# A third bank for the first layer, cutoff tests on ScalarE, and search counts summed by TensorE

## The chip, the cores and the metric

The kernel runs on one core of a Trainium2 chip. The core has TensorE (PE, matrix multiply; its weight loads are listed as PEld), VectorE (DVE), ScalarE (ACT), GpSimd (POOL) and SyncE (SP, which only issues DMAs here). PSUM, where TensorE leaves its results, is used as eight banks of 128 x 512 floats. The metric is the device time of one execution in microseconds (us); less is better. Three runs of the kernel before gave 1374.98, 1375.17 and 1376.15 us.

## What is computed

```python
def _attn_ref(x, weight):                 # x: 8 x 3584 x 192, weight: 8 heads x 7 taps
    w = softmax(weight, axis=-1)
    # causal sum over the 7 last positions, one set of taps for each group of 24 columns
    out = np.einsum('hk,bskhg->bshg', w, x_unf)

def _moe_ref(x, w_gate, w1, w2):          # x: 28672 x 192, 8 experts, F = 1024
    logits = x @ w_gate
    order = np.argsort(-logits.flatten())
    for idx in order:                     # greedy, best logit first
        tok, e = idx // E, idx % E
        if assigned[tok] >= 0 or counts[e] >= cap:   # cap = 3584
            continue
        assigned[tok] = e
        counts[e] += 1
    for e in range(E):
        mask = assigned == e
        h = np.maximum(x[mask] @ w1[e], 0.0)
        out[mask] = h @ w2[e]
```

All values are float32. Every expert gets exactly 3584 tokens, seven tiles of 512, so there are 56 tiles for the two layers.

## The kernel before

**Stages.** First comes the convolution over sixteen half batches (`conv`, `logits`), until about 205 us. After it `FFN.run` (L1321) computes the 56 tiles, and the assignment of tokens to experts is worked out piece by piece beside both.

**One tile.** Tile i goes through eight steps f. In each, `l1` (L1234) makes one block of the hidden layer in a PSUM bank `ph` by five matmuls; ScalarE writes its rounded positive part `hh`, and VectorE the remainder `hl` from the same bank, which is then free. Between the blocks `l2` (L1253) multiplies the `hh` and `hl` of the tile before with the second weights into a bank `y`; `store` (L1267) takes it out by ScalarE (`yt`) and VectorE (`yo`), and POOL scatters it. There are two banks for `ph`, two for `y`, two (`bg`) for the assignment, and two (`pa`, `pd`) for transposed tokens: eight in all.

**Tokens of a tile.** `gather` (L1201) fetches them two tiles ahead. While the assignment isn't finished, `prep` (L1310) has TensorE transpose them in steps 2 and 3 (`transp`, L1211, each call half of the blocks of both banks), and `evac` (L1224) splits them into high and low parts in steps 4 and 5. For a tile that is prepared when the assignment is done (`free`), `shuffle` (L1281) does it on VectorE.

**Assignment.** `half(0)` finds a first threshold and the lists for the first tiles; `half(1)` the second half's lists; `rest` (L1397) takes `open`, then `rounds` (L685), `final` (L803) and the `lists` for the three experts of `ib0`; `last` makes the lists of the other tiles. `rounds` runs seven entries of `ROUNDS` (L283). Each calls `choose` (L659), which tests each logit against a cutoff per expert (eight VectorE operations of 256 columns, one per expert, L668) and picks the best expert left. Then five of the seven rounds search the cutoffs in two passes: a 0/1 table of 8 experts x n thresholds x `nmax` candidates is made, its candidates are added up on VectorE by halving, and one matmul with a matrix of ones adds the partitions (L740 to L755). `choose` runs once more in `final`, so eight times in all.

**What sets the order.** Every engine's order is the program's order, laid down while the kernel is built. The assignment's pieces are Python generators, run one after the other. `Steps.hook` (L92) is called four times in each step f, and puts up to four pieces into the program at that place, unless a running estimate (`Pace`, `Meter`) says that VectorE is more than `slack`, or ScalarE more than `act`, ahead of TensorE, or that the piece waits for an estimated time (`PEW`: VectorE's estimate plus 0.8). In `FFN.run` these bounds are `SS = (0.65, 2)` (L1544).

**Points where the order is forced.** The tiles come as: eight first tiles, one of each expert; sixteen more by the lists `ia`; from tile 24 on by `ib0`, and from tile 27 on by `ib`. A list must be complete in the program before the gather that uses it, two tiles ahead. So `idx_of` (L1528) calls `bg.drain(1)` before tile 24's gather, at the head of i = 22, and `bg.drain()` at the head of i = 25: all pieces that are left up to there are put into the program at once, with no tile between them.

Of the kernel before, what the change touches and what calls it, by code (L numbers as in the profile page):

```python
# [5 lines left out]
F32 = mybir.dt.float32  # L6
BF = mybir.dt.bfloat16
I32 = mybir.dt.int32
FR = mybir.dt.float32r
AF = mybir.ActivationFunctionType  # L10
OP = mybir.AluOpType
AX = mybir.AxisListType
PSUM = bass.MemoryType.PSUM

NE, D, NTOK, F, CAP = 8, 192, 28672, 1024, 3584
W, HW_, NHB = 112, 16, 16
G = 256
# [94 lines left out]
def build(ctx, tc, nc, x, weight, wg, attn, LT, wk):  # L112
# [147 lines left out]
    def logits_t(i):  # L260
# [10 lines left out]
        if not last:  # L271
            V.tensor_tensor(o, o, v[:, 1], op=OP.add)

    k.load, k.conv, k.transp, k.split, k.logits, k.logits_t = load, conv, transp, split, logits, logits_t
    k.toeplitz, k.gate_ops, k.transp_last, k.logits_last = toeplitz, gate_ops, transp_last, logits_last
    return k
# [17 lines left out]
class Route:  # L294
# [364 lines left out]
    def choose(self):  # L659

        V, wk = self.nc.vector, self.wk
        L, t = self.LT, self.t
        us = self.u = [wk.tile([128, 4, G], F32, name="X0"), wk.tile([128, 4, G], F32, name="X1")]
        mu = self.mu = wk.tile([128, G], F32, name="c_mu")
        T = wk.tile([128, 8], F32, name="c_T")
        V.tensor_scalar(T, t, -1.0, None, op0=OP.mult)
        for e in range(8):
            V.scalar_tensor_tensor(us[e // 4][:, e % 4], L[:, e], T[:, e:e + 1], L[:, e], op0=OP.is_lt, op1=OP.subtract)  # L668
            if e % 2:
                yield  # L670
        m = wk.tile([128, 4, G], F32, name="X2")
        for q in range(2):
            V.tensor_tensor(m[:, 2 * q:2 * q + 2], us[0][:, 2 * q:2 * q + 2], us[1][:, 2 * q:2 * q + 2], op=OP.min)
            yield
        V.tensor_tensor(m[:, 0:2], m[:, 0:2], m[:, 2:4], op=OP.min)
        yield
        V.scalar_tensor_tensor(mu, m[:, 0], 0.5, m[:, 1], op0=OP.min, op1=OP.min)
        yield
        nw = self.nw = wk.tile([128, 8, G], BF, name="X2")
        for q in range(4):  # L680
            V.tensor_tensor(nw[:, 2 * q:2 * q + 2], us[q // 2][:, 2 * (q % 2):2 * (q % 2) + 2],
                            mu[:, None, :].to_broadcast([128, 2, G]), op=OP.not_equal)
            yield

    def rounds(self, sched=ROUNDS):  # L685


        nc, wk, cst = self.nc, self.wk, self.cst
        V, A, PE = nc.vector, nc.scalar, nc.tensor
        t = self.t = cst.tile([128, 8], F32, name="T")  # L690
        self.Ts2 = cst.tile([128, 1], F32, name="Ts2")
        V.tensor_scalar(self.Ts2, self.Ts, 1.5, None, op0=OP.mult)
        V.memset(t, 0.25)
        x = wk.tile([128, 8], F32, name="r_x")
# [3 lines left out]
        for parts, beta, exact, nmax in sched:  # L698
# [3 lines left out]
            for q in range(4):  # L702
                for e in range(2 * q, 2 * q + 2):
                    A.activation(wk.tile([128, G], BF, name="a_d"), self.nw[:, e], AF.Copy, accum_out=c[:, e:e + 1])
                u = self.u[q // 2][:, 2 * (q % 2):2 * (q % 2) + 2]
# [13 lines left out]
            ps = self.bg()  # L719
# [8 lines left out]
            if parts:  # L728

                V.tensor_tensor(tl, t, self.Ts2.to_broadcast([128, 8]), op=OP.min)  # L730
                V.tensor_scalar(d, tl, self.Ts, beta, op0=OP.add, op1=OP.mult)
                n = parts - 1
                jd = wk.tile([128, 2, 8, 15], F32, name="X1")[:, :, :, 0:n]
                dd = wk.tile([128, 2, 8], F32, name="r_dd")
                for s in range(2):
                    V.tensor_scalar(dd[:, s], d, float(parts) ** -(s + 1), None, op0=OP.mult)
                    V.tensor_tensor(jd[:, s], self.j1[:, None, 0:n].to_broadcast([128, 8, n]),
                                    dd[:, s, :, None].to_broadcast([128, 8, n]), op=OP.mult)
                yield
                for s in range(2):  # L740
                    th = wk.tile([128, 8, 15], F32, name="m_f")[:, :, 0:n]
                    V.tensor_tensor(th, tl[:, :, None].to_broadcast([128, 8, n]), jd[:, s], op=OP.subtract)
                    g = wk.tile([128, 8, 15, 16], BF, name="X0")[:, :, 0:n]
                    V.tensor_tensor(g[:, :, :, 0:nmax], k[:, :, None, :].to_broadcast([128, 8, n, nmax]),
                                    th[:, :, :, None].to_broadcast([128, 8, n, nmax]), op=OP.is_gt)
                    yield
                    m = nmax // 2
                    while m > 1:
                        V.tensor_tensor(g[:, :, :, 0:m], g[:, :, :, 0:m], g[:, :, :, m:2 * m], op=OP.add)
                        m //= 2  # L750
                    cc = wk.tile([128, 8, 15], BF, name="r_cc")[:, :, 0:n]
                    V.tensor_tensor(cc, g[:, :, :, 0], g[:, :, :, 1], op=OP.add)
                    yield PEW
                    ps = self.bg()[:, 0:8 * n].rearrange("p (e j) -> p e j", j=n)
                    PE.matmul(ps, self.ones, cc, start=True, stop=True)  # L755
                    ok = wk.tile([128, 8, 15], F32, name="m_x")[:, :, 0:n]
                    V.tensor_tensor(ok, ps, x[:, :, None].to_broadcast([128, 8, n]), op=OP.is_le)
                    no = wk.tile([128, 8], F32, name="r_no")
                    V.tensor_reduce(no, ok, axis=AX.X, op=OP.add)
                    V.tensor_tensor(no, no, dd[:, s], op=OP.mult)  # L760
                    V.tensor_tensor(tl, tl, no, op=OP.subtract)
            wl, xr = w[:, :, 0:8], x8
            if parts:
                g = wk.tile([128, 8, 16], BF, name="r_g2")
                V.tensor_tensor(g[:, :, 0:nmax], k, tl[:, :, None].to_broadcast([128, 8, nmax]), op=OP.is_gt)
                cc = wk.tile([128, 8], BF, name="r_c8")
# [6 lines left out]
                ps = self.bg()  # L773
# [15 lines left out]
            ps = self.bg()  # L789
# [8 lines left out]
            ps = self.bg()  # L798
# [42 lines left out]
class General:  # L841
# [9 lines left out]
    def consts(self):  # L851
# [39 lines left out]
        V.tensor_scalar(self.c31, self.c31, 31, None, op0=OP.logical_shift_left)  # L891
        self.T = p.tile([128, 8], F32, name="g_T")
        V.memset(self.T, -3.4028234663852886e38)
        self.I = p.tile([128, 8], F32, name="g_I")
# [8 lines left out]
    def choose(self):  # L903
# [9 lines left out]
        for e in range(8):  # L913
            T, I = self.T[:, e:e + 1], self.I[:, e:e + 1]
            V.tensor_scalar(c, self.id, I, None, op0=OP.is_le)
# [169 lines left out]
class FFN:  # L1085
# [122 lines left out]
                in_offset=bass.IndirectOffsetOnAxis(ap=idx[b], axis=0),  # L1208
                bounds_check=rows - 1, oob_is_err=False)

    def transp(self, i, u):  # L1211

        x = self.XG[i]
        if u == 0:
            self.pa = self.pt.tile([128, 512], F32, name="pa")
            self.pd = self.pt.tile([128, 512], F32, name="pd")
        for b in (2 * u, 2 * u + 1):
            q = slice(128 * b, 128 * b + 128)
            self.nc.tensor.transpose(self.pa[:, q], x[:, b, 0:128], self.ident)
            self.nc.tensor.transpose(self.pd[0:64, q], x[:, b, 128:D], self.ident)  # L1220
        if u:
            self.XG.pop(i)

    def evac(self, i, u):  # L1224

        A, V = self.nc.scalar, self.nc.vector
        if u == 0:
            self.XT[i] = (self.xs.tile([128, 2, 512], FR, name="xa"), self.xs.tile([128, 512], FR, name="xd"))
        xa, xd = self.XT[i]
        hi, lo, p = ((xa[:, 0], xa[:, 1], self.pa), (xd[0:64], xd[64:128], self.pd[0:64]))[u]  # L1230
        A.activation(hi, p, AF.Copy)
        V.tensor_tensor(lo, p, hi.bitcast(F32), op=OP.subtract)

# [76 lines left out]
    def prep(self, i, step):  # L1310

        if i in self.free:
            if step < 7:
                self.shuffle(i, step)
            return
        if step == 2 or step == 3:
            self.transp(i, step - 2)
        elif step == 4 or step == 5:
            self.evac(i, step - 4)

    def run(self, idx_of, at, eng, free):  # L1321

# [29 lines left out]
def moe_kernel(ctx, tc, x, weight, wg, w1, w2, out):  # L1352
    nc = Pace(tc.nc)
    V, P = nc.vector, nc.gpsimd
# [4 lines left out]
    with ExitStack() as cw:  # L1359
        pool = lambda c, name, bufs, **kw: c.enter_context(tc.tile_pool(name=name, bufs=bufs, **kw))  # L1360
        late = dict(reuse_waits="tile")
        right = dict(side="right")
        wk = pool(cw, "wk", 1)
# [4 lines left out]
        r = Route(tc, nc, LT, lst, wk, drm)  # L1368
        r.oh_pool = oh
        r.bg = lambda: bgp.tile([128, 512], F32, name="bg")  # L1370
        ff = FFN(tc, nc, attn, w1, w2, out, r.ident, wr, drm)
# [10 lines left out]
        tiles, n = [], 0  # L1382
# [44 lines left out]
        cs, c1, ct, ca, cl, cc = (ExitStack() for _ in range(6))  # L1427
# [72 lines left out]
        cx[0].close()  # L1500
        cc.close()
        ff.pt = pool(cw, "pt", 1, space=PSUM, **right, **late)
        ff.ph = pool(cw, "ph", 2, space=PSUM, **right, **late)
        bg.drain(5)
        nc.lat, nc.las = (0.8, 1.2)
        gather()
        bg.keep = 0
        ff.xs = pool(cw, "fx", 2, **late)
        for u in range(2):
            ff.transp(0, u)  # L1510
        for u in range(2):
            ff.evac(0, u)
        for _ in range(2):
            ff.wsplit(-1, P)
# [26 lines left out]
                bg.drain()  # L1541
            return [ib[:, e, 4 * (t - 3) + b:4 * (t - 3) + b + 1] for b in range(4)]

        SS = (0.65, 2)  # L1544
        ff.bg = lambda: bg.hook(SS[0], 4, SS[1])

        def at(i):
# [41 lines left out]
```

## Time and profile before

| | |
|---|---|
| median of three runs | 1375.17 us |
| the profiled execution: its time, its span | 1377.14 us, 1375.2 us |
| busy: PE, PEld, DVE | 1288.4, 1106.8, 1046.1 us |
| busy: ACT, POOL | 586.0, 637.0 us |
| mean granted clock of TensorE | 0.964 of full speed |
| HBM read, written | 114.44 MB, 72.35 MB |

Engines work beside each other, so the busy times are not to be added. A busy PE is not one at its peak: its matmuls overlap, and their ends are modelled. Tables by window give, for each stretch of the span, the busy time of each engine with the number of its instructions in brackets, then the granted clock (1.00 is full), the share of the DMA engines and the GB/s. Rows of a timeline begin with start and length, both in us; a bracket at their end is the idle time before them with what ended it. Groups end with busy us, mean ns, and, behind the bar, idle time before them.

### The profile page before, as it was taken

What the parts mean: (1) busy time and instruction counts of PE and PEld (TensorE: products, weight loads), DVE (VectorE), ACT (ScalarE), POOL (GpSimd) and SP (SyncE); (2) the same over time, 40 slices, a digit from 0 to 9 for tenths busy, and PEclk for the clock granted to TensorE, in tenths of its full rate; (3) what the DMA queues carried; (4) which work ended last, traced back from release to release, by engine and by line L of the source; (5) the groups of instructions that cost most, each with busy time, mean ns of one, the idle gap of its engine ahead of it and who ended that gap; (6) DMA issues with size and microseconds to landing.
All of it is one profiled execution on the core that took longest, in us unless ns stands there. A gap on an engine that the chain in (4) does not pass through costs nothing.

```text
span 1375.2 us, 20862 instructions
## 1 busy us (share of the span) xinstructions
PE 1288.4 (94%) x7367; PEld 1106.8 (80%) x7367; DVE 1046.1 (76%) x2216; ACT 586.0 (43%) x1242; POOL 637.0 (46%) x607
## 2 busy tenths in 40 slices
PE   5978897998989999999959999999999999999997
PEld 2545564887879989889848999999999999999997
DVE  7598963777988888888877477777777777777772
ACT  4755473447544434434413433333333333333332
POOL 5655566556754443443403344444444444444432
PEclk9998897999999999999959999999999999999999
DMA  9996568677872443343312152324231414141110
GB/s 231 284 271 166 170 218 286 204 231 248 260 260 83 143 137 97 138 143 118 100 60 81 32 197 89 101 89 139 86 99 49 140 44 146 45 142 42 42 35 28
DMA packets 114431, 188.23 MB, mean 137 GB/s; under 512 B 12352, under 2 KB 86544, under 8 KB 110096
## 3 DMA queue, kind: packets, MB, share of 16 engines
q1 hardware_dynamic: 63888, 120.75, 27.6%
q0 software_dynamic: 21504, 44.07, 10.3%
q10 hardware_dynamic: 28928, 22.02, 4.9%
q8 instruction: 59, 0.97, 0.3%
q14 instruction: 52, 0.43, 0.1%
HBM read 114.44 MB, written 72.35 MB: 136 GB/s over the span
## 4 chain that ended last, share of the span: by engine, by line
PE 74%; DVE 14%; DMA 4%; issue 3%; ACT 2%; POOL 2%; SPq 0%; POOLq 0%; DVEq 0%; ACTq 0%
PE ph L53 34%; PE y L53 32%; PE bg L53 4%; DVE X L53 4%; DMA attn<-a 2%; DVE oa L53 2%; DVE aT L53 2%; PE cv L53 1%; DVE hl L53 1%; DMA raw<-in_moe_w_dram 1%; POOL xg L1206 1%; PE pl L53 1%; DVE TH L53 1%; PE pd L53 1%; ACT hi L53 1%
## 5 line engine op out<-in xcount | busy, mean ns | idle before, releaser
L53 PE MATMUL y<-w,hh 128*128 128x384 f32 x1792 | 541.7, 358 | 0.0
L53 ACT ACTIVATE hh<-ph 128x512 fp32r<-128x512 f32 x448 | 267.7, 598 | 508.7 <-PE ph L53 377.6
L53 DVE SCALAR_TENSOR_TENSOR hl<-ph,hh 128x512 fp32r<-128x512 f32 x448 | 308.5, 689 | 196.6 <-ACT hh L53 163.7
L53 PE MATMUL y<-w,hl 128*128 128x192 f32 x1792 | 450.3, 251 | 0.0
L53 PE MATMUL ph<-xa,w 128*128 128x512 f32 x1344 | 401.7, 407 | 17.3 <-DVE hl L53 13.3
L53 PEld LDWEIGHTS y<-w,hl 128*128 128x128 f32 x1792 | 342.8, 191 | 15.4
L53 PEld LDWEIGHTS y<-w,hh 128*128 128x128 f32 x1792 | 338.4, 189 | 17.1
L1274 POOL DMA_INDIRECT out_dram<-yo,ib x128 | 126.9, 992 | 294.9 <-DVE yo L53 279.5
L53 PEld LDWEIGHTS ph<-xa,w 128*128 128x128 f32 x1344 | 221.4, 191 | 42.2 <-DVE hl L53 16.4
L1274 POOL DMA_INDIRECT out_dram<-yo,ia x96 | 107.4, 1118 | 240.6 <-DVE yo L53 202.6
L53 DVE STREAM_TRANSPOSE xs<-xg 32x256 f32<-32x256 f32 x480 | 176.9, 369 | 8.3
L53 PE MATMUL ph<-xd,w 128*128 128x512 f32 x448 | 179.2, 400 | 0.0
L53 PE MATMUL ph<-xd,dl 128*128 128x512 f32 x448 | 176.0, 393 | 0.0
L1206 POOL DMA_INDIRECT xg<-attn,ib x128 | 130.1, 1016 | 70.2 <-issue 69.9
L226 POOL TENSOR_TENSOR lo<-aT,hi 128x768 fp32r<-128x768 f32 x50 | 93.3, 1896 | 73.5 <-ACT hi L53 73.5
L53 PE MATMUL cv<-X,TH 118*128 118x384 f32 x256 | 106.6, 548 | 19.2 <-DVE TH L53 12.8
L1206 POOL DMA_INDIRECT xg<-attn,ia x96 | 105.2, 1096 | 28.8 <-issue 27.6
L53 ACT ACTIVATE yt<-y 128x192 f32<-128x192 f32 x224 | 73.4, 328 | 97.5 <-PE y L53 87.5
L53 DVE TENSOR_TENSOR yo<-y,yt 128x192 f32<-128x192 f32 x224 | 79.6, 355 | 45.6 <-ACT yt L53 42.4
L53 PEld LDWEIGHTS cv<-X,TH 118*128 118x128 f32 x256 | 50.4, 210 | 65.2 <-issue 14.8
L53 PEld LDWEIGHTS ph<-xd,w 128*128 128x128 f32 x448 | 85.2, 190 | 21.3 <-issue 2.2
L53 PEld LDWEIGHTS ph<-xd,dl 128*128 128x128 f32 x448 | 85.1, 190 | 19.9 <-POOL dl L1187 0.3
(241 smaller groups left out, 1233.5 us busy)
## 6 DMA issues: line engine op xcount, KB each, us to landing
w<-kw SPq DMA_DIRECT2D x16, 1536.0 KB
w<-kv SPq DMA_DIRECT2D x16, 1536.0 KB
X<-in_x_dram SPq DMA_DIRECT2D x16, 1344.0 KB
attn<-a ACTq DMA_DIRECT2D x16, 1344.0 KB
kw<-w SPq DMA_DIRECT2D x48, 256.0 KB
kv<-w SPq DMA_DIRECT2D x32, 384.0 KB
raw<-in_moe_w_dram SPq DMA_DIRECT2D x32, 192.0 KB
raw<-in_moe_w_dram SPq DMA_DIRECT2D x16, 256.0 KB
```

The costliest lines, as they stand in the source:

```text
L53: return f(*a, **k)
L226: eng.tensor_tensor(lo, aT, hi.bitcast(F32), op=OP.subtract)
L1206: self.nc.gpsimd.indirect_dma_start(out=t[:, b], out_offset=None, in_=self.attn[0:rows], in_offset=bass.IndirectOffsetOnAxis(ap=idx[b], ax ...
L1274: st = nc.gpsimd.indirect_dma_start(out=self.out, out_offset=bass.IndirectOffsetOnAxis(ap=idx, axis=0), in_=o, in_offset=None, bounds_chec ...
```

## The change

The banks: `pa` and `pd` become one bank `px`, used for the first 128 columns of all four blocks (step 1, out in step 2) and then for the other 64 (step 4, out in step 5); `ph` gets three banks. The cutoff tests: ScalarE takes the sign of logit plus (negative) cutoff into a bf16 table, and two VectorE operations of 1024 columns do what eight of 256 did; the estimate of VectorE is set to ScalarE's before each. The search: the adds by halving are left out, and `nmax` matmuls (16 in the first round, 8 in the other four that search), each over one candidate of the table, add into the bank. The bounds of the hook become `(1.8, 3)`.

```diff
@@ choose
         mu = self.mu = wk.tile([128, G], F32, name="c_mu")
-        T = wk.tile([128, 8], F32, name="c_T")
-        V.tensor_scalar(T, t, -1.0, None, op0=OP.mult)
+        sg = wk.tile([128, 8, G], BF, name="X2")
         for e in range(8):
-            V.scalar_tensor_tensor(us[e // 4][:, e % 4], L[:, e], T[:, e:e + 1], L[:, e], op0=OP.is_lt, op1=OP.subtract)
+            self.nc.scalar.activation(sg[:, e], L[:, e], AF.Sign, bias=t[:, e:e + 1])
             if e % 2:
                 yield
+        for q in range(2):
+            self.nc.dve = max(self.nc.dve, self.nc.act)
+            h = slice(4 * q, 4 * q + 4)
+            V.scalar_tensor_tensor(us[q], sg[:, h], 0.0, L[:, h], op0=OP.is_lt, op1=OP.subtract)
+            yield
@@ rounds
-                    yield
-                    m = nmax // 2
-                    while m > 1:
-                        V.tensor_tensor(g[:, :, :, 0:m], g[:, :, :, 0:m], g[:, :, :, m:2 * m], op=OP.add)
-                        m //= 2
-                    cc = wk.tile([128, 8, 15], BF, name="r_cc")[:, :, 0:n]
-                    V.tensor_tensor(cc, g[:, :, :, 0], g[:, :, :, 1], op=OP.add)
                     yield PEW
                     ps = self.bg()[:, 0:8 * n].rearrange("p (e j) -> p e j", j=n)
-                    PE.matmul(ps, self.ones, cc, start=True, stop=True)
+                    for m in range(nmax):
+                        PE.matmul(ps, self.ones, g[:, :, :, m], start=(m == 0), stop=(m == nmax - 1))
@@ transp
-    def transp(self, i, u):
+    def transp(self, i, u, bank=None):
         x = self.XG[i]
-        if u == 0:
-            self.pa = self.pt.tile([128, 512], F32, name="pa")
-            self.pd = self.pt.tile([128, 512], F32, name="pd")
-        for b in (2 * u, 2 * u + 1):
+        p = self.px = bank or self.pt.tile([128, 512], F32, name="px")
+        for b in range(4):
             q = slice(128 * b, 128 * b + 128)
-            self.nc.tensor.transpose(self.pa[:, q], x[:, b, 0:128], self.ident)
-            self.nc.tensor.transpose(self.pd[0:64, q], x[:, b, 128:D], self.ident)
+            if u == 0:
+                self.nc.tensor.transpose(p[:, q], x[:, b, 0:128], self.ident)
+            else:
+                self.nc.tensor.transpose(p[0:64, q], x[:, b, 128:D], self.ident)
@@ evac
-        hi, lo, p = ((xa[:, 0], xa[:, 1], self.pa), (xd[0:64], xd[64:128], self.pd[0:64]))[u]
+        hi, lo, p = ((xa[:, 0], xa[:, 1], self.px), (xd[0:64], xd[64:128], self.px[0:64]))[u]
@@ prep
-        if step == 2 or step == 3:
-            self.transp(i, step - 2)
-        elif step == 4 or step == 5:
-            self.evac(i, step - 4)
+        if step in (1, 4):
+            self.transp(i, step // 4)
+        elif step in (2, 5):
+            self.evac(i, step // 5)
@@ moe_kernel
-        ff.ph = pool(cw, "ph", 2, space=PSUM, **right, **late)
+        ff.ph = pool(cw, "ph", 3, space=PSUM, **right, **late)
...
         for u in range(2):
-            ff.transp(0, u)
-        for u in range(2):
+            ff.transp(0, u, r.bg() if u else None)
             ff.evac(0, u)
...
-        SS = (0.65, 2)
+        SS = (1.8, 3)
```

## The prediction

> **What bounds the kernel now.** I read the busy table in 40 slices first, then windows of 25 us, then the timeline of TensorE and VectorE where these dip, and at last the groups and waits.
>
> ```profile
> PE   5978897998989999999959999999999999999997
> PEclk9998897999999999999959999999999999999999
> ```
>
> Counted from 0, from slice 12 on (413 us) TensorE is at 9 in nearly all slices, at full clock; one dip stands out, slice 20, with PEclk 5. By windows (PE, PEld, DVE, ACT, POOL with counts, then clock, DMA share, GB/s):
>
> ```profile
> 675.00:700.00 25.00, 17.25 (x115) 14.54 (x112) 21.47 (x51) 5.91 (x13) 5.37 (x5) 0.85 0.31 99
> 700.00:725.00 25.00, 18.02 (x194) 16.30 (x195) 16.88 (x46) 5.31 (x8) 2.20 (x3) 0.53 0.02 5
> ```
>
> ```profile
> 688.75 0.25 PE L53 MATMUL y<-w,hl 128*128 128x192 f32 x1
> 693.66 0.26 PE L53 MATMUL bg<-ones,F 128*128 128x1 bf16 x4 [4.67 <-DVE F L53]
> ...
> 704.25 4.88 PE L53 MATMUL bg<-X,oa 128*128 128x16 bf16 x64 [6.37 <-DVE oa L53]
> ...
> 720.60 1.63 PE L53 MATMUL ph<-xa,w 128*128 128x512 f32 x3
> ...
> 724.86 0.95 PE L53 MATMUL ph<-xa,w 128*128 128x512 f32 x3
> ```
>
> The last matmul of the two layers ends at 689.0, the next begins at 720.6: a **hole of 31.6 us** in which TensorE has only small `bg` matmuls. That is the forced point at the head of i = 22: what `rest` hasn't put into the program by then is done with no tile beside it. What was left then:
>
> ```profile
> 341.19 0.47 DVE L53 TENSOR_SCALAR c_T<-T 128x8 f32<-128x8 f32 x1
> ...
> 415.74 0.16 DVE L53 TENSOR_SCALAR c_T<-T 128x8 f32<-128x8 f32 x1
> ...
> 463.50 0.16 DVE L53 TENSOR_SCALAR c_T<-T 128x8 f32<-128x8 f32 x1
> ...
> 647.13 0.19 DVE L53 TENSOR_SCALAR c_T<-T 128x8 f32<-128x8 f32 x1
> ...
> 678.99 0.17 DVE L53 TENSOR_SCALAR c_T<-T 128x8 f32<-128x8 f32 x1
> ...
> 688.77 0.43 DVE L53 SCALAR_TENSOR_TENSOR c_mu<-X 128x256 f32<-128x256 f32 x1
> ...
> 696.74 0.16 DVE L53 TENSOR_TENSOR bad<-bad,u_s 128x1 f32<-128x1 f32 x1
> ...
> 721.33 0.68 DVE L53 SCALAR_TENSOR_TENSOR X<-bg,F 128x512 f32<-128x512 f32 x1
> ...
> 770.41 0.29 DVE L53 SCALAR_TENSOR_TENSOR ib<-m_j,m_x 128x128 int32<-128x128 int32 x1
> ```
>
> A `c_T` (eight in all; five shown) opens each `choose`. The eighth, of `final`, is at 679.0; its checks end at 696.9, and then a whole set of lists was made before TensorE came back. The next set, which begins at 721.3 and ends with `ib` at 770.4, had tiles beside it and took 49 us. So the seven rounds, from 341 to 679, are what is late; a round that searches lasts 463.5 - 415.7 = 47.8 us, one that doesn't 679.0 - 647.1 = 31.9.
>
> What limits a round? VectorE. In the steady stretch from 425 to 675 us it is the third column of the window's row, 213.0 busy and 37 idle; below stand the groups of VectorE and ScalarE in the same stretch:
>
> ```profile
> 425.00:675.00 250.00, 248.95 (x1465) 223.44 (x1465) 213.03 (x507) 109.98 (x273) 110.49 (x101) 1.00 0.36 122
> ```
>
> ```profile
> L53 DVE SCALAR_TENSOR_TENSOR hl<-ph,hh 128x512 fp32r<-128x512 f32 x101 | 69.5, 688 | 25.5 <-ACT hh L53 19.6 <-issue 5.5
> L53 DVE TENSOR_TENSOR yo<-y,yt 128x192 f32<-128x192 f32 x51 | 18.0, 353 | 3.1 <-ACT yt L53 2.4 <-issue 0.3
> L53 DVE SCALAR_TENSOR_TENSOR X<-LT,c_T 128x256 f32<-128x256 f32 x40 | 16.9, 478 | 0.2
> L53 DVE TENSOR_TENSOR xd<-pd,xd 64x512 fp32r<-64x512 f32 x13 | 8.9, 685 | 0.4
> L53 DVE TENSOR_TENSOR xa<-pa,xa 128x512 fp32r<-128x512 f32 x12 | 8.2, 679 | 0.0
> L53 DVE TENSOR_TENSOR X<-X 128x480 bf16<-128x480 bf16 x8 | 3.4, 420 | 0.1
> L53 DVE TENSOR_TENSOR X<-X 128x240 bf16<-128x240 bf16 x8 | 3.3, 413 | 0.3
> L53 DVE TENSOR_TENSOR r_cc<-X 128x120 bf16<-128x120 bf16 x8 | 3.2, 402 | 0.3
> ```
>
> ```profile
> L53 ACT ACTIVATE hh<-ph 128x512 fp32r<-128x512 f32 x101 | 60.4, 598 | 115.7 <-PE ph L53 94.7 <-issue 11.3 <-PE pd L53 9.4
> L53 ACT ACTIVATE yt<-y 128x192 f32<-128x192 f32 x51 | 16.9, 331 | 23.1 <-PE y L53 20.5 <-issue 1.0 <-DVE X L53 0.5
> ```
>
> The tiles take 69.5 + 18.0 + 8.9 + 8.2 = 104.6 us of it, so the assignment gets 108.4 in 250, a share of 0.434. Of the 37 idle, 25.5 stand before `hl` and 3.1 before `yo`: VectorE had run out of background pieces and stood until ScalarE handed over. The 101 `hl` are 12.6 tiles, 19.8 us each.
>
> **Part 1, the hook's bounds (1.8, 3).** With 1.8 us of VectorE work placed ahead, it should find background work where it now stands before `hl`. I give back two thirds of the 28.6 us (ends: none, all): the assignment gets 108.4 + 19 = 127.5, a factor 1.176.
>
> **Part 2, the search.** Per search round go 2 x (0.420 + 0.413 + 0.402) = 2.5 us of VectorE. TensorE gets 2 x 16 + 4 x 2 x 8 = 96 matmuls for 10.
>
> ```profile
> L53 PE MATMUL bg<-r_cc,ones 128*128 128x120 bf16 x8 | 1.8, 227 | 0.0
> ```
>
> ```profile
> 724.44 0.22 PE L53 MATMUL bg<-ones,tot 128*128 128x128 bf16 x1
> ...
> 724.83 0.22 PE L53 MATMUL bg<-U,tot 128*128 128x128 bf16 x1
> ```
>
> Eight matmuls of 128 columns in bf16, each with its own weights, start from 724.44 to 724.83, seven distances of 0.056 us. So +86 x 0.056 = **+4.8 us**, on the bounding engine. No row has this reading pattern, one value every 32 bytes. The ends are nothing beyond 0.056, and the 0.227 that a lone one lasts, 86 x 0.227 = 19.5. I take the former, as the nearer row is one of such a chain.
>
> [...]
>
> **Part 3, the cutoff tests.** VectorE loses 8 x 0.478 + 0.21 = 4.0 us per `choose` and gets two operations of 1024 columns; rows of that size:
>
> ```profile
> L53 DVE SCALAR_TENSOR_TENSOR F<-X,F 128x1024 bf16<-128x1024 bf16 x2 | 2.4, 1219 | 0.0
> L53 DVE TENSOR_TENSOR LT<-LT,c_mu 128x1024 f32<-128x1024 f32 x2 | 4.4, 2182 | 0.0
> L53 ACT ACTIVATE a_d<-LT,b 128x256 bf16<-128x256 f32 x16 | 8.1, 507 | 0.4
> ```
>
> The same kind of operation takes 1.22, so 2.4; the upper end is 4.4. ScalarE gets eight Signs at 0.507 = 4.1 us, on an engine that is 44% busy in that stretch (110.0 of 250). But VectorE must wait for them, and `hl` and `yo` of the tiles queue behind it; `hh` and `yt` queue behind the Signs, which themselves wait for the cutoffs that VectorE writes. I put this at 1.5 us of standing per `choose` (ends: none, 4.1), so part 3 gives VectorE about 0.1 us net. At TensorE I add 8 x 0.4 = **+3 us** for blocks whose `hl` comes too late (ends 0, and 8 x 1.5 = 12).
>
> **Sum for the rounds.** A search round holds 47.8 x 0.434 = 20.7 us of background VectorE; it becomes 20.7 - 2.6 = 18.1, so 47.8 x (18.1 / 20.7) / 1.176 = 35.5, 12 less; one without search 31.9 / 1.176 = 27.1, 5 less. Five and two: 70 us, so `final` starts near 679 - 70 = 609. It needs about 30 us beside tiles (18 us without, 679.0 to 696.9) and the lists 49, or some 42 at the better rate: done at about 681, just at the forced point (689, a few us earlier). **The hole closes.** Its matmuls don't vanish:
>
> ```profile
> 736.29 2.12 PE L53 MATMUL bg<-X,oa 128*128 128x16 bf16 x32
> ```
>
> 32 sort matmuls beside tiles cost 2.12 us, 0.066 each; 128 of them are 8.5, and the 65 other small ones of the hole at 0.06 another 4. So the hole gives **31.6 - 12.5 = -19 us**. If `final` were 20 us later, 20 us of mixed work would be drained in 20 x 31.6 / 79 = 8 us, 5 of them lost; I charge **+2** for that edge. The three matmuls at 720.6 took 1.63 against 0.95 at 724.9: slow clock after the hole, **-1** over the first block.
>
> **Part 4, the banks.**
>
> ```profile
> PE ph L53 <- DVE hl L53: 13.3, 9, 3.3
> ```
>
> The first layer stood 13.3 us, nine times, for `hl` to free its bank. Every bank is now held one step f longer, 19.8 / 8 = 2.5 us, which covers all but a little of the longest, 3.3. But a wider bound lets VectorE be 1.15 us further behind, so I take half: **-6** (ends 0, -13). That cover is what makes part 1 harmless; without it each `hl` 1.15 us later would meet a stall.
>
> For the transposes, eight per tile are the same work, one step earlier. One bank in place of two means that those of step 4 wait for step 2's copies: two steps, 5 us, are enough. They use no DMA, and the gather they read was issued a tile earlier.
>
> ```profile
> 675.07 0.27 PE L53 MATMUL pa<-ident,xg 128*128 128x128 f32 x1
> 675.18 0.27 PE L53 MATMUL pd<-ident,xg 128*64 128x128 f32 x1
> ```
>
> 0.11 us each, 0.88 per tile. The assignment now ends at 770; with `last`'s 42 to 49 us behind 681 it ends near 725, two to three tiles earlier, which VectorE then shuffles instead: **-2**. Also, counts that TensorE takes before VectorE's real backlog is done: **+2** (ends 0, 18; the waits for `bg` inputs are few now since VectorE catches up while it stands).
>
> Sum: -19 + 2 - 1 - 6 + 4.8 + 3 - 2 + 2 = -16. The sum is made on the profiled execution, 1377.1 us (span 1375.2 and 1.9 around it): 1361. The runs' median is 2 lower, 1375.2, which gives **1359**.
>
> **Rivals.**
>
> *The hole only shrinks.* VectorE gets back none of its idle time: a search round is 47.8 x 18.1 / 20.7 = 41.8, six less, the others are unchanged, and `final` starts 30 us earlier. Then 649 + 30 + 49 - 686 = 42 us of mixed work is left at the forced point: 17 of hole, 10 of them lost, 8 beyond my edge: 1367. For it: the Signs and the waits for counts stop VectorE however much work lies ahead.
>
> *VectorE's backlog reaches TensorE.* The estimate takes 0.613 us for an `hl` that lasts 0.688; before, VectorE caught up while it stood before `hl`. If the 1.8 takes this away, matmuls of the search and of `ph` wait: 25 waits for counts (five in each round that searches) and eight `choose`, at 0.5 us some 17 us where the sum has 2. Result 1374: no change.
>
> *The strided reads are slow.* If each of the 86 takes the lone one's 0.227, TensorE pays 19.5 in place of 4.8: 1374. Against it: those 0.227 are mostly latency, since the rows of the chain of eight last 0.22 too and start 0.056 apart. [...]
>
> *Slower: the Signs block VectorE.* In each `choose` VectorE stands for eight Signs with an `hh` and a `yt` between them, 4.1 + 0.6 + 0.3 = 5.0 us, and does 2.4: 7.4 against 4.0, so a round gets 3.4 longer, more than the search gives; with part 1's gain lost beside it, `final` starts at 679 as now and the hole stays. TensorE pays the search 4.8 and eight stalls of 5 + 1.2 + 0.7 less the cover of 5, some 2 each, 15; the bank gives 6 back: 1375 + 14 = 1389. It decides where the standing eats more than 10 us a round, what parts 1 and 2 give. Against it: ScalarE is 44% busy, and the hook lets it be 3 us ahead before more is placed.
>
> That the change doesn't do what it says: the bounds are tied to an estimate, so that VectorE stands as before; this is the first rival's price.
>
> **How the numbers follow.** Chances: forecast 0.54 (its own range 1345 to 1367), shrunken hole 0.18, backlog 0.09, strided reads 0.05, Signs block 0.10; 0.04 for better than 1345, where the stalls of part 4 go whole (-7) and lists and clock before 425 us gain too. The range leaves out the slower case and the far end of this one: 1343 to 1377. A measurement can tell 0.2% (2.75 us): faster is below 1372.4. From the cases: forecast and better 0.58, shrunken hole 0.16, backlog 0.04 and reads 0.02 make 0.80; same 0.10; slower 0.10.
>
> **What would show it.** Right: no stretch of over 5 us without `y` matmuls between 650 and 730; `final`'s Signs near 609, where its `c_T` is now at 679; VectorE over 90% busy from 425 on until then. Part 1 is wrong if `hl` still has 25 us idle before it in 250; part 2 if the 8 search matmuls take over 0.6 us together; part 3 if the two wide operations show idle before them of over 1.5 us each time; part 4 if `ph` still waits 13 us for `hl`. The whole is wrong if the hole is as long as now.

## The result, and the profile after

| | before | after |
|---|---|---|
| median, beside each other on one chip | 1375.92 us | 1367.96 us |
| ratio, 95% interval | | 0.9948 (0.9932 to 0.9964) |
| profiled span | 1375.2 us | 1366.2 us |
| mean granted clock | 0.964 | 0.978 |

The forecast was 1359; of the 16 us that it summed, 8 came. One execution of a kernel below (e11) took 1417.72 us, far above its others, and is left out of its ratio. The page's table in 40 slices, of after:

```profile
PE   5887897999999999999999999999999999999997
PEclk9998898999999999999999999999999999999999
```

Slice 20 is 9 in both rows. The windows show the same (PE, PEld, DVE, ACT, POOL with counts, clock, DMA share, GB/s); the first row is a stretch that lies wholly within the rounds, of which before's own follows:

```profile
425.00:600.00 175.00, 175.00 (x1012) 152.26 (x1012) 139.76 (x321) 84.01 (x212) 74.21 (x65) 1.00 0.32 107
675.00:700.00 25.00, 24.88 (x240) 21.72 (x240) 16.80 (x44) 8.81 (x16) 5.82 (x5) 0.93 0.18 62
700.00:725.00 25.00, 25.00 (x213) 22.62 (x212) 21.13 (x45) 8.79 (x17) 7.80 (x8) 1.00 0.31 109
```

```profile
425.00:600.00 175.00, 174.43 (x1027) 156.76 (x1027) 147.91 (x351) 76.16 (x188) 78.09 (x71) 1.00 0.36 119
```

TensorE is busy for 24.88 and 25.00 of 25 us where it had 17.25 and 18.02. The longest stretch without a matmul of the two layers between 640 and 780 us is now 2.0 us: **the hole of 31.6 us is gone**. How it closed is in the timelines of ScalarE (first and last cutoff test), VectorE (last list) and POOL (first gather by `ib`, at the head of i = 22), and that gather before:

```profile
320.57 3.31 ACT L53 ACTIVATE X<-LT,T 128x256 bf16<-128x256 f32 x8
636.94 2.51 ACT L53 ACTIVATE X<-LT,T 128x256 bf16<-128x256 f32 x6 [2.08 <-DVE T L53]
737.33 0.29 DVE L53 SCALAR_TENSOR_TENSOR ib<-m_j,m_x 128x128 int32<-128x128 int32 x1
724.10 1.04 POOL L1204 DMA_INDIRECT xg<-attn,ib  x1 [0.31 <-PE ph L53]
```

```profile
722.19 1.04 POOL L1206 DMA_INDIRECT xg<-attn,ib  x1 [30.08 <-issue]
```

The first test stands 20.6 us earlier (341.2 to 320.6), since bounds and banks also hurry what comes before the rounds (e7 and e6 below, with one of them each, have the first test at 323.6 and 330.4); the rounds take 316.4 us where they took 337.8. So `final` is 42 us earlier, not 70, and that suffices. But the gather is issued at 724.1 where it was at 722.2: up to there nothing is won, although no hole lies before it. All of the gain comes later, where the last list had still been made until 770.4, now 737.3 (1375.2 - 722.2 = 653.0 us from the gather to the end, now 642.1). TensorE has got more to do before the gather. First, the search's matmuls:

```profile
L53 PE MATMUL bg<-X,ones 128*128 128x120 bf16 x64 | 15.2, 395 | 0.0
L53 PE MATMUL bg<-X,ones 128*128 128x56 bf16 x32 | 3.6, 282 | 2.6 <-DVE X L53 2.6
```

```profile
386.16 1.81 PE L53 MATMUL bg<-X,ones 128*128 128x56 bf16 x16
387.74 0.47 PE L53 MATMUL ph<-xd,w 128*128 128x512 f32 x1
...
431.70 1.90 PE L53 MATMUL bg<-X,ones 128*128 128x120 bf16 x8
433.25 0.53 PE L53 MATMUL y<-w,hh 128*128 128x384 f32 x1
```

Eight search matmuls of 120 columns hold TensorE from 431.70 to 433.25, 1.55 us or 0.194 each, where I had 0.056; sixteen of 56 columns take 1.58, 0.099 each. All: 64 x 0.194 + 32 x 0.099 = **15.6 us**, less 10 x 0.056 for the old ones: +15 in place of +4.8.

Second, work has moved ahead of the gather: between 205 us and it, TensorE now does 356 of the 512 sort matmuls (`bg<-X,oa`) where it did 256, beside as many matmuls of the two layers. At the 0.066 each of the prediction's row these 100 are 6.6 us, an estimate; so more than half of what is won behind the gather is work that was done earlier.

VectorE stands more than before. In 425 to 600 its busy time fell from 147.9 to 139.8, so idle rose from 27.1 to 35.2. Its groups there, after:

```profile
L53 DVE SCALAR_TENSOR_TENSOR hl<-ph,hh 128x512 fp32r<-128x512 f32 x67 | 45.9, 684 | 12.6 <-ACT hh L53 12.4
L53 DVE TENSOR_TENSOR yo<-y,yt 128x192 f32<-128x192 f32 x33 | 11.6, 352 | 6.3 <-ACT yt L53 5.9
L53 DVE SCALAR_TENSOR_TENSOR X<-X,LT 128x1024 f32<-128x1024 bf16 x8 | 9.7, 1218 | 3.5 <-ACT X L53 3.5
L53 DVE TENSOR_TENSOR m_x<-bg,r_x 128x120 f32<-128x120 f32 x8 | 2.3, 284 | 8.2 <-PE bg L53 8.2
```

Idle before `hl` is 12.6 (before: 18.0), but 6.3 before `yo`, 3.5 before the wide tests (for the Signs) and 8.2 before `m_x`, which takes the search's counts: eight waits of a microsecond for slow matmuls (in e1 below, where the matmuls are fast, 0.9 in all). At last TensorE's waits:

```profile
PE ph L53 <- DVE hl L53: 4.0, 3, 2.2
PE px L53 <- DVE xa L53: 3.5, 5, 1.1
```

13.3 became 4.0, and the one bank for transposes brings 3.5.

### The profile page after: what moved, and what is told of

Read it like the earlier page. It is cut to its first block, busy times and chain, and to the rows that moved or that the text cites. A ratio compares the mean times of both kernels' runs of the same rounds, so it can differ in the third digit from the quotient of the medians.

```text
span 1366.2 us, 21041 instructions
## 1 busy us (share of the span) xinstructions
PE 1293.3 (95%) x7437; PEld 1106.1 (81%) x7437; DVE 1032.9 (76%) x2160; ACT 608.9 (45%) x1306; POOL 645.2 (47%) x607
## 4 chain that ended last, share of the span: by engine, by line
PE 76%; DVE 13%; DMA 4%; ACT 3%; issue 1%; POOL 1%; SPq 0%; POOLq 0%; DVEq 0%; ACTq 0%
PE ph L53 34%; PE y L53 33%; PE bg L53 5%; DVE X L53 4%; DMA attn<-a 2%; DMA raw<-in_moe_w_dram 2%; DVE aT L53 2%; DVE oa L53 2%; PE cv L53 2%; PE px L53 1%; DVE hl L53 1%; PE pl L53 1%; DVE TH L53 1%; ACT hi L53 1%; POOL w L1185 1%
## 5 line engine op out<-in xcount | busy, mean ns | idle before, releaser
L53 PEld LDWEIGHTS y<-w,hl 128*128 128x128 f32 x1792 | 342.8, 191 | 15.6 <-DVE hl L53 0.4
L53 PEld LDWEIGHTS y<-w,hh 128*128 128x128 f32 x1792 | 338.1, 189 | 17.2 <-issue 0.2
L1272 POOL DMA_INDIRECT out_dram<-yo,ia x96 | 113.3, 1181 | 246.9 <-DVE yo L53 218.7
L53 DVE STREAM_TRANSPOSE xs<-xg 32x256 f32<-32x256 f32 (+1 forms) x512 | 188.8, 369 | 8.8
L1204 POOL DMA_INDIRECT xg<-attn,ia x96 | 109.1, 1137 | 28.8 <-issue 23.3
L53 PEld LDWEIGHTS cv<-X,TH 118*128 118x128 f32 x256 | 49.1, 205 | 65.8 <-ACT a L53 17.5
```

Source lines behind the costliest of these rows:

```text
L53: return f(*a, **k)
L1204: self.nc.gpsimd.indirect_dma_start(out=t[:, b], out_offset=None, in_=self.attn[0:rows], in_offset=bass.IndirectOffsetOnAxis(ap=idx[b], ax ...
L1272: st = nc.gpsimd.indirect_dma_start(out=self.out, out_offset=bass.IndirectOffsetOnAxis(ap=idx, axis=0), in_=o, in_offset=None, bounds_chec ...
```

## Experiments

Ratios are to the kernel before, run on the same chip. **e1** turns the search table, so that the 120 values of a matmul lie side by side; e2, e3 and e4 each undo one part of the change.

```diff
-g = wk.tile([128, 8, 15, 16], BF, name="X0")[:, :, 0:n]
+g = wk.tile([128, 16, 8, 15], BF, name="X0")[:, 0:nmax, :, 0:n]
...
-PE.matmul(ps, self.ones, g[:, :, :, m], start=(m == 0), stop=(m == nmax - 1))
+PE.matmul(ps, self.ones, g[:, m], start=(m == 0), stop=(m == nmax - 1))
```

> The changed kernel with the search's 0/1 table turned: candidate first, so that each of the search matmuls reads 120 (or 56) values that lie side by side in place of one every 32 bytes. Nothing else differs. Theory S (the strided reads are what ate the gain): in the changed kernel eight search matmuls of 120 columns hold TensorE 1.55 us, 0.194 each, and sixteen of 56 columns 1.58, 0.099 each; side by side they should start about 0.056 apart, so TensorE gets back 64 x 0.138 + 32 x 0.045 = 10 us: 1358. Rival B (VectorE's backlog and its standing behind the Signs ate it; the slow matmuls are waits): the matmuls stay at 0.19 or their time turns up as idle before them: 1366 to 1369.

1360.48 us, 0.9885 (0.9867 to 0.9903). The timeline of its TensorE:

```profile
388.99 0.66 PE L53 MATMUL bg<-X,ones 128*128 128x56 bf16 x16
389.49 0.48 PE L53 MATMUL ph<-xd,w 128*128 128x512 f32 x1
...
430.66 0.59 PE L53 MATMUL bg<-X,ones 128*128 128x120 bf16 x8
431.07 0.42 PE L53 MATMUL y<-w,hh 128*128 128x384 f32 x1
```

Eight take 0.41 us, 0.051 each; sixteen of 56 columns 0.50, 0.031 each (below, "full speed" stands for these two). Same number of matmuls and of values: it is where the values lie. The time is the forecast's, and some 2 us above what I expected of this run.

**e2**, the search of before (adds on VectorE, one matmul) put back:

> The changed kernel with the search as it was: adds by halving on VectorE and one matmul per pass; banks, cutoff tests and bounds stay changed. Theory S: TensorE gets back 15.6 us of strided matmuls less 0.6; VectorE gets 2.5 us more work in each of five rounds, so the last cutoff test comes at 650 in place of 637, some 13 us of list work may be drained alone (3 us lost): 1356 to 1359. Rival B: more work for VectorE makes its backlog worse: 1370 or more.

1363.77, 0.9912 (0.9895 to 0.9928): better than the change, less so than I expected, and worse than e1 on the same chip, by 3.7 us by the ratios (uncertain by 3.4).

**e3**, the cutoff tests of before put back on VectorE:

> The changed kernel with the cutoff tests as they were, eight operations of 256 columns on VectorE and none on ScalarE. Theory S: the tests matter little: VectorE gets 1.4 us more work per choose but no longer stands 2 to 3 us behind the Signs, so a round is within 2 us of the changed kernel's and the time is 1365 to 1369. Rival B: standing behind the Signs is the loss; without it hl comes in time, rounds get 3 us shorter, and the time is 1360 or less.

1367.73, 0.9943 (0.9931 to 0.9955), as the change. Its last cutoff test:

```profile
617.78 0.17 DVE L53 TENSOR_SCALAR c_T<-T 128x8 f32<-128x8 f32 x1
```

It is 19 us earlier than after's 636.9, and the ratio is the same within what can be told (some 3 us, since the two were measured apart): once the hole is closed, finishing the rounds sooner brings nothing that shows here.

**e4**, `SS = (0.65, 2)` with all the rest of the change:

> The changed kernel with the hook's bounds as they were (0.65, 2). Theory S: the wide bounds are what brought the first cutoff test from 341 to 321 and shortened the rounds, so with the narrow ones the last test comes at 660 or later, part of the lists is drained with no tile beside it, and the time is 1372 to 1378. Rival: the bounds do nothing once the other parts are in; the hole stays closed: 1366 to 1369.

1377.48, 1.0013 (1.0004 to 1.0022). The edges of the stretch without layer matmuls, on its TensorE's timeline:

```profile
696.35 0.25 PE L53 MATMUL y<-w,hl 128*128 128x192 f32 x1
...
722.64 1.63 PE L53 MATMUL ph<-xa,w 128*128 128x512 f32 x3
```

From 696.6 to 722.6 the hole is back, 26.0 us. So the bounds close it; the other parts together, the slow reads among them, gain nothing. Both bounds were moved together here and in e7, so which of them does it is not shown.

**e6, e7, e8**, with search and cutoff tests of before: the banks alone (`SS` at 0.65, 2), the bounds alone (two `ph` banks, `pa` and `pd` as before), and both.

> The kernel before with the banks alone: one for transposed tokens, three for the first layer, transposes in steps 1 and 4. Bounds (0.65, 2), search and cutoff tests as before. Theory (the bounds do the work, the bank only makes them harmless): the 13.3 us of waits of the first layer for hl shrink to 4, the transposes wait some 2 us for their one bank, and the hole at the forced point stays: 1366 to 1373. Rival (the bank itself is the gain): the rounds begin earlier too, the hole shrinks: 1360 or less.

> The kernel before with the bounds (1.8, 3) alone, the first layer still with two banks. Theory: the hole closes or nearly so (19 us), but with hl up to 1.15 us later and two banks the first layer waits for hl more than the 13.3 us of before, by 10 to 25 us: 1365 to 1382. Rival (two banks are enough): waits stay at 13 us and the time is 1358 or less.

> The kernel before with banks and bounds, search and cutoff tests as before. Theory: these two are the gain and the other two parts are a loss (search, 10 us) and nothing (cutoff tests): the hole closes but for some 5 us, since the search's adds are back on VectorE: 1360 to 1365, below the changed kernel. Rival (the search and the tests are needed to close the hole): 1370 or more.

e6: 1366.81, 0.9943 (0.9928 to 0.9957). e7: 1361.6, 0.9906 (0.9891 to 0.9921). e8: 1359.22, 0.9886 (0.9865 to 0.9906). On that chip the kernel before took 1374.85: -8.0, -13.3 and -15.6, so the parts don't add. In e6 the hole stays, 25.6 us from 686.4 on, as its theory said. In e7 the longest stretch without a layer matmul between 640 and 780 us is 2.3 us: the bounds alone close the hole. The time of e7 lies between its two expectations, that of e8 just below its own. TensorE's waits between 205 and 760 us, of e7 and then of e8:

```profile
PE ph L53 <- DVE hl L53: 14.7, 14, 2.5
PE bg L53 <- DVE r_cc L53: 4.5, 1, 4.5
PE bg L53 <- ACT oa L53: 0.7, 1, 0.7
PE bg L53 <- DVE oa L53: 0.2, 1, 0.2
```

```profile
PE ph L53 <- DVE hl L53: 2.2, 2, 1.7
PE bg L53 <- DVE r_cc L53: 7.8, 4, 5.6
PE bg L53 <- ACT oa L53: 4.9, 1, 4.9
PE bg L53 <- DVE oa L53: 3.5, 4, 1.6
```

With two banks, bounds of 1.8 leave the waits for `hl` at 14.7, against 13.3: nothing had to make the bounds harmless. The third bank takes 12.5 of them away, but the waits for background operands, `r_cc` (the old search's added table) and `oa`, grow from 5.4 to 16.2: what TensorE doesn't lose to the layers it loses to the background, which it reaches sooner. The longest of them shows it: the first `bg` transpose of `oa` begins at 235.51 in e7 after 0.68 us of waiting, and at 233.04 in e8 after 4.87. (The profiled execution of e8 was its slowest, 1363.47, and that of e7 took 1362.48, so these two traces account for the waits and not for the 2.4 us between the medians.) VectorE in the stretch within the rounds, e7 and e8:

```profile
425.00:600.00 175.00, 174.85 (x1033) 156.50 (x1030) 157.93 (x394) 76.97 (x188) 78.60 (x72) 1.00 0.35 118
```

```profile
425.00:600.00 175.00, 173.92 (x1026) 155.32 (x1024) 156.79 (x391) 75.50 (x186) 76.51 (x72) 1.00 0.36 119
```

157.9 and 156.8 busy of 175: idle 17.1 and 18.2, where before had 27.1. The bounds do fill VectorE's idle time, by about ten of 27.

**e9**: banks, bounds, the turned table of e1, and the cutoff tests left on VectorE.

> The changed kernel with the turned table of e1 and the cutoff tests on VectorE as before. Theory: the tests' place moves the last test some 15 us earlier (617.8 against 636.9 in e3 and the changed kernel), but the hole is closed already, so only a transposed tile or two are saved: as e1, 1358 to 1361. Rival (rounds that end sooner pay on): 1355 or less.

1355.08, **0.9861 (0.9843 to 0.9878)**, the best of all, below what I expected and at the rival's 1355. VectorE's timeline (first and last cutoff test), and a wait of TensorE between 205 and 760 us:

```profile
322.49 0.17 DVE L53 TENSOR_SCALAR c_T<-T 128x8 f32<-128x8 f32 x1
...
604.90 0.17 DVE L53 TENSOR_SCALAR c_T<-T 128x8 f32<-128x8 f32 x1
```

```profile
PE bg L53 <- DVE X L53: 3.8, 4, 2.0
```

`final` is at 604.9, where I had forecast 609. In e1 it is at 627.0; e9 is 3.3 us faster by the ratios, but on another chip, so whether rounds that end sooner still pay is left open by this pair. TensorE waits 3.8 us for the search's table in place of 7.8 for `r_cc`.

**e5**: the table laid out anew in each round that searches, so that the values of one matmul lie 32, 16, 8, 4 and 2 bytes apart in rounds one to five.

```diff
-g = wk.tile([128, 8, 15, 16], BF, name="X0")[:, :, 0:n]
+S = (16, 8, 4, 2, 1)[r]
+g = wk.tile([128, 1920], BF, name="X0")[:, 0:nmax * 8 * n].rearrange(
+    "p (a e j b) -> p a e j b", a=nmax // S, e=8, j=n)
...
+PE.matmul(ps, self.ones, g[:, m // S, :, :, m % S], start=(m == 0), stop=(m == nmax - 1))
```

> The changed kernel with another distance between the values that a search matmul reads in each of the five searching rounds: 32, 16, 8, 4 and 2 bytes (the candidates are cut into groups, so VectorE makes the table in 1, 1, 2, 4 and 8 operations). [...] Rival (the price grows evenly with the distance): 16 bytes about half of 32, 8 bytes a quarter. The sum of the time isn't the point here.

One execution, 1372.38. TensorE's timeline, each eight search matmuls and the instruction behind them (16, 8, 4 and 2 bytes):

```profile
432.81 1.87 PE L53 MATMUL bg<-X,ones 128*128 128x120 bf16 x8
434.34 0.58 PE L53 MATMUL ph<-xd,w 128*128 128x512 f32 x1
...
476.39 1.03 PE L53 MATMUL bg<-X,ones 128*128 128x120 bf16 x8
477.18 0.42 PE L53 MATMUL y<-w,hh 128*128 128x384 f32 x1
...
517.29 0.60 PE L53 MATMUL bg<-X,ones 128*128 128x120 bf16 x8
517.70 0.42 PE L53 MATMUL y<-w,hh 128*128 128x384 f32 x1
...
564.02 0.59 PE L53 MATMUL bg<-X,ones 128*128 128x120 bf16 x8
564.42 0.48 PE L53 MATMUL ph<-xd,w 128*128 128x512 f32 x1
```

1.53, 0.79, 0.41 and 0.40 us for eight. So of the five distances 2 and 4 bytes took the same time, 8 about twice that and 16 nearly four times, and 32 no more than 16 (1.55 above). The even growth that the rival expected doesn't hold: 16 bytes took as long as 32, not half, and 8 took half as long as 32, not a quarter.

**e10, e11**: e9 with `SS` of (2.6, 4) and of (1.2, 3).

> The kernel of e9 (turned table, cutoff tests on VectorE, three banks) with the bounds at (2.6, 4). Theory (VectorE's last cutoff test at 605 already leaves 80 us before the forced point, the rest is TensorE): no gain, 1354 to 1358, with some more waits for hl. Rival (more work ahead keeps shortening the rounds): 1352 or less.

> The kernel of e9 with the bounds at (1.2, 3). Theory: the last test comes some 15 to 20 us later, at about 622, still before the point where the hole opens: 1355 to 1359. Rival (the bounds pay in proportion): 1362 or more.

1370.9, 0.993 (0.9903 to 0.9956), and 1368.75, 0.9916 (0.9902 to 0.9931). Both are worse than I expected, and neither is better than e9. Their traces agree: between 205 and 760 us TensorE is idle for 31.9 us in e10 and 28.4 in e11, for 22.7 in e9 and 24.1 in the same kernel as e9 on a further chip (e16 below). So bounds on either side of (1.8, 3) look worse, by some 6 to 9 us by the ratios; since no chip ran all of them, how much stays open.

**e12**: the change with each search matmul issued twice, the first time into an unused half of the bank.

```diff
+for m in range(nmax):
+    PE.matmul(p2, self.ones, g[:, :, :, m], start=(m == 0), stop=(m == nmax - 1))
```

> The changed kernel with each of the 96 search matmuls issued twice, the first time into an unused half of the bank. Theory S (the strided matmuls stand on the path that sets the end): 64 x 0.194 + 32 x 0.099 = 15.6 us more, 1381 to 1385. Rival (they fill time in which TensorE would wait for VectorE anyway): less than 5 us more.

1393.54, 1.0105 (1.009 to 1.0119), more than expected. So I ran the pair again on one chip, with the change itself (e13), the doubled change (e14), e1 with its matmuls doubled (e15) and e9 (e16).

> The changed kernel itself, as the base of this call's chip: ratio to the kernel before 0.993 to 0.996.

> The changed kernel with each of the 96 search matmuls issued twice, as e12, on this call's chip. Theory S: the second set's own 15.6 us and some 2 us of longer rounds: 16 to 18 us above e13. Rival (a strided matmul also costs what waits behind it): 20 us or more, as e12.

> The turned table of e1, with each of the 96 matmuls issued twice. Theory S (the stride costs, not the number): the second set costs 64 x 0.05 + 32 x 0.03 = 4 us, so it stays 4 to 6 us below e13, which has half as many matmuls. Rival (it is the number of small matmuls between the tiles' that costs): as e13 or above it.

> The kernel of e9 (turned table, cutoff tests on VectorE) on the same chip as e13. If the tests on ScalarE took a part of the missing gain, it is 11 us or more below e13 (8 of the search and 3); if not, 7 to 9 us.

| | us | ratio |
|---|---|---|
| e13, the change | 1375.49 | 0.9976 (0.9964 to 0.9987) |
| e14, doubled | 1395.32 | 1.0121 (1.01 to 1.0143) |
| e15, turned table, doubled | 1365.8 | 0.9891 (0.9868 to 0.9915) |
| e16, as e9 | 1360.87 | 0.987 (0.9849 to 0.9891) |

TensorE in e14 and in e15, one pass of the search and what follows it:

```profile
436.00 3.65 PE L53 MATMUL bg<-X,ones 128*128 128x120 bf16 x16
439.30 0.71 PE L53 MATMUL ph<-xd,w 128*128 128x512 f32 x1
```

```profile
430.30 1.01 PE L53 MATMUL bg<-X,ones 128*128 128x120 bf16 x16
431.13 0.48 PE L53 MATMUL ph<-xd,w 128*128 128x512 f32 x1
```

Sixteen take 3.30 us at 32 bytes and 0.83 side by side. e15 issues twice as many matmuls as the change and is 9.7 us faster: not their number costs, but how they read. (I had expected 4 to 6 us.) Without its second passes (8 x 0.42 + 2 x 0.50 = 4.4 us, an estimate from these rows) the difference would be 14. Doubling the slow ones costs 19.8 us, where eight passes of 3.30 - 1.55 and two of 1.58 make 17.2; the other 2 to 3 are not located, so e14 lies between its theory and its rival. e16 is 14.6 us below e13, more than the 11 that were to show a price of the Signs; but e15 less its second passes stands level with e16 and has the Signs, so on this chip the reads account for the difference. On this chip the change is worth 0.9976, less than I expected, on the first 0.9948; the intervals just touch.

## Why the prediction came out so

**The step that failed** is part 2's "So +86 x 0.056 = **+4.8 us**, on the bounding engine". The chain of eight at 0.056 was a row of matmuls that read side by side; these read one value every 32 bytes and cost 0.194 and 0.099, +15 in all. The sign that I had named for it, over 0.6 us for eight, came at 1.55. I had both ends, took the nearer row by kind of chain, and gave the upper end 0.05. What differed between the row and the case was the very thing that set the price: with the table turned and nothing else, the same matmuls cost 0.051 and 0.031 (e1).

The experiments give each term, from the ratios of neighbours that differ in one part (times some 1375 us; a single ratio is uncertain by 2 to 2.5 us, a difference of two by 3 to 4):

| term | forecast | measured | from |
|---|---|---|---|
| bounds: hole -19, edge +2, clock -1, early counts +2, fewer transposed tiles -2 | -18 | -13 | e7 |
| banks | -6 | -3 | e8 less e7 |
| search, read at full speed | +4.8 | -3 | e9 less e8 |
| Signs (cutoff tests on ScalarE) | +3 | +3 | e1 less e9 (two chips) |
| sum with full-speed reads | -16 | -16 | e1 |
| reads of 32 bytes' step | 0 | +9 to +14 | after less e1 (measured apart); e13 less e15 and its second passes (one chip) |
| all | -16 | -7 (the medians: -8) | after |

The measured terms are steps of one chain (e7, e8, e9, e1, the change), so they add up by themselves, and another order would share them out otherwise, as the banks' -8 alone shows. The reads' own time beyond full speed is 15.6 - 64 x 0.051 - 32 x 0.031 = 11.3, between the two figures. So the sum came out for the kernel that I had in mind, which is e1, but in part by luck: the bounds brought some 5 us less than forecast and the banks 3 less, the search read at full speed 8 more. The threes of the table can't, each by itself, be told from nothing; that the search did not cost the 4.8 that I had charged can be told.

**Banks.** Wait for wait I was near: 13.3 to 4.0 is -9.3, less 3.5 for `px`. Alone they give -8 (e6). Beside the bounds they give little, since TensorE then waits for the background instead (e7, e8). The fewer transposed tiles come with the bounds: 26 in the kernel before (104 transposes into `pa`), 24 in e7, in e8 and in the change. And "That cover is what makes part 1 harmless" is wrong: with two banks the bounds cost 14.7 - 13.3 = 1.4 us of waits.

**Search at full speed.** I charged TensorE its matmuls, but nothing for the adds on VectorE that it no longer waits for. e8 waits 7.8 us for `r_cc`, e9 3.8 for the table. e1 less e2, on one chip, gives -3.7, so the sign is seen twice. That the adds make it is argued from the waits, not tried by itself.

**The hole.** Closed, by the bounds, as forecast (e4, e7). Its worth, with its side terms, was 13 rather than 18. Between 205 and 760 us, TensorE in the kernel before and in e7:

```profile
205.00:760.00 555.00, 516.65 (x3207) 452.61 (x3205) 440.20 (x968) 239.56 (x553) 263.09 (x239) 0.95 0.49 161
```

```profile
205.00:760.00 555.00, 530.06 (x3308) 464.35 (x3309) 452.62 (x1010) 247.88 (x569) 272.25 (x243) 0.96 0.49 162
```

Idle went from 38.3 to 24.9, 13.4 us, which is what the time shows. In the hole itself TensorE had been idle for 7.75 + 6.98 = 14.7 of 31.6 us (its two windows) and busy with the small matmuls for the rest; the forecast let these shrink to 12.5 beside tiles, and whether they did is not shown.

**The rounds.** `final` is at 637, not 609, and VectorE is 80% busy (139.8 of 175), not over 90%. Part 1's own sign (25 us of idle before `hl` in 250) would call it wrong: it is 24.3 there. But e7 and e8 are 90% busy: the bounds do fill VectorE, and the Signs and the slow counts empty it again (of the 175, e1, with Signs and fast counts, is idle 32.9, e3, with slow counts and no Signs, 27.1, e9, with neither, 17.5). That `final` came 28 us later than forecast cost little that shows, since the hole closes with 42 us as it does with 61 (e3).

**Signs.** The wide operations wait 3.5 us for eight, 0.4 each, below my 1.5, but `yo` and `hl` wait too. Their price is +3.3 by e1 less e9 and +3.6 by e2 less e8, all across two chips; by after less e3 it is +0.7, and on the last chip nothing, since e15 is 4.9 us above e16 and its second passes alone are 8 x 0.42 + 2 x 0.50 = 4.4. So the +3 is neither shown nor refuted. The rival that they turn the change slower was wrong.

**Rivals.** The result's 1368 is the shrunken hole's figure (1367), but only by luck, since the hole closed. What came is the strided reads, whose 1374 was too far: they hold TensorE for 15 us, not 19.5, and with 15 the sum would have given 1369. The backlog didn't come: in the change TensorE waits 4.0 us for `hl` and 2.6 for the search's table, where that rival had 17 for the two.

## What to carry to other kernels

A row prices an operation only if it reads its operands in the same pattern (here the row's 0.056 us stood for matmuls that took 0.194); where no row has the pattern, lay the data out so that one does (here by the order of the table's axes; VectorE's operation that writes 960 of it takes 1158 ns either way). Work that ends just before a forced point is worth hurrying up to that point; beyond it, e3 shows no gain, and e9 against e1 leaves room for a few us. And when two changes shorten waits of the same engine, expect less than their sum (here -8.0 and -13.3 made -15.6), as the engine moves on to the next thing that is late (in e8 TensorE's waits for background operands, 16.2 us where e7 had 5.4).

## What the runs showed of the hardware

The distances of e5, one execution, both passes of each round alike: in the search's bf16 matmuls of 120 columns, values 4 bytes apart took no longer than 2 apart (0.051 us a matmul against 0.050), 8 apart about twice that (0.099), 16 nearly four times (0.191), and 32 no longer than 16 (0.194, in the change). And the price is not read from an instruction's listed duration: the mean is 0.395 us at 32 bytes and 0.218 side by side (the groups of after and of e1), less than a factor two, where the distance from the first of a chain of eight to the instruction behind it, 1.55 against 0.41 us, differs by nearly four.
